# Softcap attention and FFN on one core: two token blocks go through the FFN in portions of 10 and 6 chunks

## The chip, the core and the metric

The kernel runs on 1 core of one Trainium2 chip. The metric is device time in microseconds (us) of one execution; the median of 3 runs of the kernel before is 713.72 us (710.97 to 714.97).

## The reference, cut to what matters

```python
# 4 batches, 12 heads, 448 positions, head size 64
scores = (q @ k.T) / sqrt(64)
scores = cap * tanh(scores / cap)              # cap = 30
attn   = exp(scores - max); attn /= attn.sum(-1) + 1e-9
x      = (attn @ v), heads side by side        # 1792 tokens x 768
h      = x @ w_in                              # w_in 768 x 2048, 64-bit floats
g      = h - tanh(h)
out    = g @ w_out                             # w_out 2048 x 768, 64-bit floats
```

The weights arrive as 64-bit floats and are decoded on the core. To keep 32-bit accuracy with fast matmuls, operands are split into a high and a low part, and a product is three matmuls (high x high, high x low, low x high).

## The kernel before, in words

The 1792 tokens are 4 blocks, one per batch, of 448 tokens; 384 of each (three tiles of 128) go through the FFN with their block, and the 64 that are left over of every block go through with block 3. The 12 heads are 6 pairs per block; a pair's attention (`prep_pair`, `scores`, `pv` or `pv_f32`, `normalize`, L513 to L890) ends in one 128-row slice of the block's transposed x. The first 11 pairs use plain 32-bit matmuls for attn @ v (`F32_PAIRS`, L32), which need no split of the exponentials; the other 13 split them.

The FFN of a block loops over 16 chunks of 128 hidden columns (`moe`, L1195). A chunk needs its weights: `prep_w` (L1070) calls `fetch_w` (L936), which in block 0 reads 1.5 MiB of raw 64-bit words (L965 and L977), decodes them with three VectorE passes (L1007, L1014, L1021) into a buffer `u`, and writes `u` to DRAM from the POOL queue (`fuk`, L951); the other blocks read `u` back, 768 KB (L944). Then `u` is split into `wi` and `wo`, each a copy (L420 on ScalarE or L422 on VectorE) and a subtraction (L431). `first` (L1109) makes 18 matmuls of 384 columns into h (L1124 to L1126), then tanh on ScalarE (L1137), h - tanh on VectorE (L1139) and a split of g. `second` (L1155) adds 18 matmuls (L1177) to the block's sums y, which stay in five PSUM banks over all its 16 chunks, with the `first` of the next chunk ahead of the `second` of this one. After the last chunk `store` (L1325) copies the sums to buffers `o` (two of them) and sends them out. `split_x` (L1084) makes the high and low parts of a block's x, `xh` and `xl`, at its first chunk; there are six buffers of each, as many as one block needs, so the next block's parts are written when the last `first` that reads the old ones is through. There are two buffers of raw words (`w64`), two of `u`, two of `wi`, three of `wo`, and six of `x`.

The order on every engine and DMA queue is written when the kernel is built: `Plan.schedule` (L119) places the operations one by one with a table of costs, prefers what can start at once, and among those the earliest due time. `emit` (L1366) gives the due times: FFN block b is due from `starts[b]`, and the attention of block b + 1 is spread over the time of FFN block b, moved ahead by `LEAD` (L34). So the attention of block 0 comes first and alone, and that of blocks 1, 2 and 3 stands between the matmuls of FFN blocks 0, 1 and 2. In blocks 2 and 3, `inspect` (L1027) reads the raw weights again to look at their range.

Of the kernel before, what the change touches and what calls it, by code (L numbers as in the profile page):

```python
# [31 lines left out]
F32_PAIRS = 11  # L32

LEAD = (18000.0, 30000.0, 20000.0, 20000.0)  # L34
# [267 lines left out]
class Build:  # L302
# [6 lines left out]
    def __init__(self, ctx, tc, q, k, v, w_in, w_out, out, consts, checks, general):  # L309
# [47 lines left out]
        self.raw, self.u, self.w, self.kept_op = {}, {}, {}, {}  # L357
        self.acc = {}
# [577 lines left out]
    def fetch_w(self, i):  # L936

        nc, DM, plan = self.nc, self.DM, self.plan
        m, f = divmod(i, self.NF)
        cols = slice(128 * f, 128 * f + 128)  # L940
        if m:
            u = plan.buf("u", [128, 2, DM])
            o = self.dma(
                "SP", 8 * 128 * DM, lambda: nc.sync.dma_start(out=u(), in_=self.u_kept[f]), [self.kept_op[f]], [u]  # L944
            )
            return u, [o]
# [123 lines left out]
    def prep_w(self, i):  # L1070

        DM = self.DM
        u, deps = self.fetch_w(i)
# [10 lines left out]
    def split_x(self, m):  # L1084
        n, plan = self.FULL, self.plan
        self.xa = []
        for d in range(self.ND):
            xh, xl = plan.buf("xh", [128, n], F32R), plan.buf("xl", [128, n], F32R)
            x, o = self.x.pop((m, d))
            ops = self.split(n, xh, xl, x, [o], ([xh], [xl]), ([x], [x, xh]))  # L1090
            self.xa.append((xh, xl, slice(0, n), ops))
        if m < self.B - 1:
            return
# [101 lines left out]
    def moe(self):  # L1195
# [4 lines left out]
        n = B * NF  # L1200
        for i in range(n + 1):
            m, f = divmod(i, NF)
            pm, pf = divmod(i - 1, NF)
            if i < n:
                self.prep_w(i)
# [5 lines left out]
                if f == 0:  # L1211
                    self.split_x(m)
                fifo[i] = []
                yield from self.first(self.w[i][0], self.xa, self.FULL, ("g", "gh", "gl"), fifo[i])
            if i > 0:
                yield from self.second(
                    self.w[i - 1][1], fifo[i - 1][0], [(0, 0), (1, 128), (2, 256)], pf == NF - 1
                )
                if pf == NF - 1:
                    self.store((0, 1) if pm == B - 1 else (0, 1, 2), pm)  # L1220
# [4 lines left out]
            if i > 0 and pm == B - 1:  # L1225
                yield from self.second(self.w[i - 1][1], fifo[i - 1][1], [(3, 0), (4, 128)], pf == NF - 1)
# [25 lines left out]
    def rest(self):  # L1252
# [3 lines left out]
        o4 = self.store((2, 3, 4), self.B - 1)  # L1256
# [68 lines left out]
    def store(self, tiles, m):  # L1325
        k = self.at + 3000
        for i in tiles:
            o = self.plan.buf({3: "eh", 4: "el"}.get(i, "o"), [128, self.DM])
            ops = []
            for bk, c0, e0, ne in self.PIECES[i]:  # L1330
                acc = self.acc[bk]
                new = not ops
                ops.append(
                    self.copy(
                        ne, lambda o=o, e0=e0, ne=ne: o()[:, e0 : e0 + ne],
# [141 lines left out]
```

## Time and profile before

| | |
|---|---|
| median of 3 runs | 713.72 us (710.97 to 714.97) |
| profiled execution, first to last instruction | 712.2 us |
| attention of block 0 alone, 0 to 78.7 us | PE busy 68.69 us of 78.70 |
| FFN block 0 with attention of block 1, to 240.4 us | PE busy 154.78 us of 161.70 |
| FFN block 1 with attention of block 2, to 387.1 us | PE busy 145.53 us of 146.70 |
| FFN block 2 with attention of block 3, to 533.9 us | PE busy 146.01 us of 146.80 |
| FFN block 3 and the left-over tokens, to the end | PE busy 172.34 us of 178.30 |

How to read the profile: PE is TensorE's matmuls, PEld its weight loads (they overlap), DVE is VectorE, ACT is ScalarE, POOL is GpSimd, SP the SyncE queue that issues most transfers; a q behind an engine's name is its queue of issues and waits. A group of instructions is named by its line, its engine and the tiles it writes and reads (`fwi<-fu` writes wi and reads u). Matmuls overlap in the records, so the distance between two starts is what one costs. The stages of the table begin with the first FFN matmul of each block. Idle time of an engine counts only where the matmuls wait for it.

### The profile page before, as it was taken

How to read it: one execution, taken by the hardware profiler on the slowest of the kernel's cores; microseconds unless marked ns; L12 is line 12 of the kernel's file. 1: busy time of each engine (PE TensorE's matmuls, PEld its weight loads, DVE VectorE, ACT ScalarE, POOL GpSimd, SP SyncE). 2: the span in 40 equal slices, each digit the busy share in tenths (PEclk: the TensorE clock that was granted, in tenths of full speed). 3: DMA queues.
4: the chain of work that ended last, by engine and by line, in shares of the span. 5: the costliest groups of instructions: out<-in, count | busy, mean ns of one | idle time of the engine just before them, and what ended most of it. 6: DMA issues, size and time to landing. Idle time of an engine off the chain costs nothing.

```text
span 712.2 us, 10004 instructions
## 1 busy us (share of the span) xinstructions
PE 687.4 (97%) x3624; PEld 603.2 (85%) x3624; DVE 515.2 (72%) x800; ACT 563.8 (79%) x961; POOL 14.3 (2%) x35
## 2 busy tenths in 40 slices
PE   6998999989999999999999999999999999999996
PEld 5655788778788888999999989899989999999996
DVE  5798999988999889877788888786694333333331
ACT  7998987848778999989989999999886655455553
POOL 2000000000000000000000000000000000000000
PEclk9999999999999999999999999999999999999999
DMA  6999899999974576653536785686676566676433
GB/s 102 152 212 194 191 285 241 225 250 243 266 263 137 111 206 172 170 125 97 120 95 176 233 205 153 157 219 180 166 212 227 154 141 167 178 166 152 133 84 116
DMA packets 156159, 125.96 MB, mean 177 GB/s; under 512 B 115268, under 2 KB 142020, under 8 KB 156100
## 3 DMA queue, kind: packets, MB, share of 16 engines
q1 hardware_dynamic: 153716, 112.58, 65.8%
q0 software_dynamic: 2304, 12.58, 4.9%
q8 instruction: 30, 0.49, 0.3%
q14 instruction: 29, 0.24, 0.1%
q10 hardware_dynamic: 80, 0.07, 0.0%
HBM read 107.12 MB, written 18.09 MB: 176 GB/s over the span
## 4 chain that ended last, share of the span: by engine, by line
PE 50%; ACT 25%; DVE 10%; DMA 10%; issue 3%; SPq 2%; DVEq 0%; ACTq 0%
PE facc L1177 16%; PE fh L1124 7%; DMA fw<-in_moe_w_in_dram 7%; PE fh L1126 7%; PE fh L1125 7%; PE fs L649 3%; ACT fqst L420 2%; ACT fe L722 2%; ACT fe L663 2%; ACT feh L663 2%; DMA fu<-fuk 2%; PE fp L790 2%; ACT fwi L420 2%; ACT feh L722 2%; ACT feh L420 2%
## 5 line engine op out<-in xcount | busy, mean ns | idle before, releaser
L1177 PE MATMUL facc<-fwo,fgh 128*128 128x512 f32 (+1 forms) x768 | 171.2, 345 | 0.0
L1177 PEld LDWEIGHTS facc<-fwo,fgh 128*128 128x128 f32 x768 | 127.4, 188 | 20.1 <-issue 5.8
L1124 PE MATMUL fh<-fxh,fwi 128*128 128x384 f32 x384 | 135.9, 354 | 0.0
L1126 PE MATMUL fh<-fxh,fwi 128*128 128x384 f32 x384 | 130.2, 339 | 0.3 <-DVE fwi L431 0.3
L1125 PE MATMUL fh<-fxl,fwi 128*128 128x384 f32 x384 | 128.8, 335 | 0.0
L1177 PE MATMUL facc<-fwo,fgl 128*128 128x512 f32 (+1 forms) x384 | 99.0, 339 | 0.0
L431 DVE TENSOR_TENSOR fwi<-fu,fwi 128x768 fp32r<-128x768 f32 x66 | 62.8, 952 | 48.8 <-ACT fwi L420 48.6
L420 ACT CAST fwi<-fu 128x768 fp32r<-128x768 f32 x62 | 51.7, 834 | 37.9 <-PE fh L1126 24.6
L1124 PEld LDWEIGHTS fh<-fxh,fwi 128*128 128x128 f32 x384 | 72.2, 188 | 5.6 <-issue 2.6
L1125 PEld LDWEIGHTS fh<-fxl,fwi 128*128 128x128 f32 x384 | 72.2, 188 | 4.5 <-issue 3.0
L431 DVE TENSOR_TENSOR fwo<-fu,fwo 128x768 fp32r<-128x768 f32 x66 | 62.6, 952 | 15.5 <-ACT fwo L420 15.1
L1126 PEld LDWEIGHTS fh<-fxh,fwi 128*128 128x128 f32 x384 | 72.0, 188 | 0.6 <-DVE fwi L431 0.6
L1139 DVE TENSOR_TENSOR fg<-fh,fg 128x384 f32<-128x384 f32 x64 | 35.6, 557 | 47.7 <-ACT fg L1137 46.7
L1177 PEld LDWEIGHTS facc<-fwo,fgl 128*128 128x128 f32 x384 | 58.7, 188 | 8.6
L649 PE MATMUL fs<-fqst,fkst 128*128 128x448 f32 x142 | 55.4, 411 | 4.7 <-DVE fkst L557 2.7
L1137 ACT ACTIVATE fg<-fh 128x384 f32<-128x384 f32 x64 | 31.2, 487 | 35.2 <-PE fh L1126 35.0
L663 ACT ACTIVATE fe<-fs 128x448 f32<-128x448 f32 x91 | 49.3, 541 | 7.7 <-PE fs L649 6.7
L431 DVE TENSOR_TENSOR fel<-fe,feh 128x896 fp32r<-128x896 f32 x39 | 42.4, 1087 | 12.3 <-ACT feh L420 12.2
L420 ACT CAST feh<-fe 128x896 fp32r<-128x896 f32 (+1 forms) x64 | 50.7, 794 | 0.6
L722 ACT ACTIVATE fe<-fe,absc 128x896 f32<-128x896 f32 (+1 forms) x52 | 49.6, 954 | 0.6
L420 ACT CAST fwo<-fu 128x768 fp32r<-128x768 f32 x56 | 46.4, 829 | 4.0 <-PE facc L1177 3.7
L649 PE MATMUL fs<-fql,fkz 128*128 128x448 f32 x124 | 45.5, 367 | 0.0
(191 smaller groups left out, 1329.6 us busy)
## 6 DMA issues: line engine op xcount, KB each, us to landing
fu<-fuk SPq DMA_DIRECT2D x48, 768.0 KB
fw<-in_moe_w_in_dram SPq DMA_DIRECT2D x64, 384.0 KB
fw<-in_moe_w_out_dram SPq DMA_DIRECT2D x32, 768.0 KB
fuk<-fu POOLq DMA_DIRECT2D x16, 768.0 KB, 5.9
fqraw<-in_q_dram SPq DMA_DIRECT2D x44, 112.0 KB
fkraw<-in_k_dram SPq DMA_DIRECT2D x44, 112.0 KB
out_dram<-fo SPq DMA_DIRECT2D x12, 384.0 KB
fvraw<-in_v_dram SPq DMA_DIRECT2D x26, 96.0 KB
```

Source lines behind the costliest of these rows:

```text
L420: self.nc.scalar.copy(out(), in_())
L431: lambda: self.nc.vector.tensor_sub(lo(), x(), hi().bitcast(F32)),
L649: nc.tensor.matmul(ps()[:, :S], k, q, start=n == 0, stop=n == passes - 1)
L663: S, lambda: nc.scalar.activation(dst(), ps()[:, :S], AF.Tanh), [o],
L722: lambda e=e, w=w: nc.scalar.activation(e()[:, :w, :], e()[:, :w, :], AF.Exp, scale=self.absc),
L790: nc.tensor.matmul(P()[:, :S], self.v_block(v1(), hp, c), e()[:, j, :], start=n == 0, stop=n == 3)
L1124: nc.tensor.matmul(h()[:, :n], wh, ah, start=(d == 0), stop=False)
L1125: nc.tensor.matmul(h()[:, :n], wh, al, start=False, stop=False)
L1126: nc.tensor.matmul(h()[:, :n], wl, ah, start=False, stop=(d == ND - 1))
L1137: n, lambda: nc.scalar.activation(g()[:, :n], h()[:, :n], AF.Tanh), [prev], [g], [h], psum=True, key=k
L1139: o = self.dve(n, lambda: nc.vector.tensor_sub(g()[:, :n], h()[:, :n], g()[:, :n]), [o], [], [g, h], key=k + 600)
L1177: nc.tensor.matmul(banks[bk]()[:, c0 : c0 + ne], lhs()[:, ts], w()[:, k, e0 : e0 + ne], start=bk in firsts and bk not in begun, stop=stop ...
```

## The change

`SEGMENTS` replaces the loop over blocks: chunks 0 to 9 of block 0, chunks 0 to 9 of block 1, chunks 10 to 15 of block 0, chunks 10 to 15 of block 1, then blocks 2 and 3 whole. Weights of chunk f are decoded where f comes up first. When block 0 or 1 leaves off after chunk 9, its sums go to DRAM (`keep_y`: the copies of `store`, then three SP transfers of 384 KB), and they come back into `o` at its end, where VectorE adds them to the sums in PSUM (`evict` with `old`). Its xh and xl are written to DRAM by 12 POOL transfers of 192 KB when they are made (`keep_x`), and read back by 12 SP transfers when it goes on (`fetch_x`). `SHARES` says beside which portions the attention is due: that of block 1 beside the first, of block 2 half beside the second and half beside the third, of block 3 beside block 2. `LEAD` has a value for each portion. The buffers are as before.

```diff
--- before.py
+++ after.py
@@ -31,7 +31,11 @@
 
 F32_PAIRS = 11
 
-LEAD = (18000.0, 30000.0, 20000.0, 20000.0)
+SEGMENTS = ((0, 0, 10), (1, 0, 10), (0, 10, 16), (1, 10, 16), (2, 0, 16), (3, 0, 16))
+
+SHARES = (None, {0: 1.0}, {1: 0.5, 2: 0.5}, {4: 1.0})
+
+LEAD = (18000.0, 40000.0, 30000.0, 30000.0, 30000.0, 30000.0)
 
 FREE_PAIRS = 8
 
@@ -355,6 +359,15 @@
         self.x, self.xt_ops = {}, {d: [] for d in range(self.ND)}
         self.raw_qk, self.ready, self.raw_v = {}, {}, {}
         self.raw, self.u, self.w, self.kept_op = {}, {}, {}, {}
+        self.segments = [(m, a, z) for m, a, z in SEGMENTS]
+        later = {m for m, a, _ in self.segments if a}
+        self.x_kept = {
+            m: [self.dram.tile([128, 2, self.FULL], F32, name=f"{nm}xk{m}_{d}") for d in range(self.ND)] for m in later
+        }
+        self.y_kept = {
+            m: [self.dram.tile([128, self.DM], F32, name=f"{nm}yk{m}_{i}") for i in range(3)] for m in later
+        }
+        self.x_ops, self.y_ops = {}, {}
         self.acc = {}
         self.at = 0.0
         if not general:
@@ -933,12 +946,10 @@
 
 
 
-    def fetch_w(self, i):
+    def fetch_w(self, f):
 
         nc, DM, plan = self.nc, self.DM, self.plan
-        m, f = divmod(i, self.NF)
-        cols = slice(128 * f, 128 * f + 128)
-        if m:
+        if f in self.kept_op:
             u = plan.buf("u", [128, 2, DM])
             o = self.dma(
                 "SP", 8 * 128 * DM, lambda: nc.sync.dma_start(out=u(), in_=self.u_kept[f]), [self.kept_op[f]], [u]
@@ -1067,10 +1078,10 @@
         o = self.plan.op("PL", 2000.0, spread, [o], key=k)
         self.plan.op("D", 70.0, put, [o], key=k)
 
-    def prep_w(self, i):
+    def prep_w(self, i, f):
 
         DM = self.DM
-        u, deps = self.fetch_w(i)
+        u, deps = self.fetch_w(f)
         made = []
         for j, tag in enumerate(("wi", "wo")):
             w = self.plan.buf(tag, [128, 2, DM], F32R)
@@ -1081,14 +1092,43 @@
             made.append((w, list(ops)))
         self.w[i] = made
 
-    def split_x(self, m):
+    def fetch_x(self, m, d):
+
+        n, plan, nc, kept = self.FULL, self.plan, self.nc, self.x_kept[m][d]
+        both = [plan.buf(t, [128, n], F32R) for t in ("xh", "xl")]
+        ops = [
+            self.dma(
+                "SP", 512 * n, lambda j=j, t=t: nc.sync.dma_start(out=t().bitcast(F32), in_=kept[:, j, :]), self.x_ops[m, d], [t],
+            )
+            for j, t in enumerate(both)
+        ]
+        return (*both, slice(0, n), ops)
+
+    def keep_x(self, m, d):
+
+        n, nc, kept = self.FULL, self.nc, self.x_kept[m][d]
+        *both, _, ops = self.xa[d]
+        self.x_ops[m, d] = [
+            self.dma(
+                "PL", 512 * n, lambda j=j, t=t: nc.gpsimd.dma_start(out=kept[:, j, :], in_=t().bitcast(F32)), [ops[j]], [], [t],
+                key=self.at + 40000,
+            )
+            for j, t in enumerate(both)
+        ]
+
+    def split_x(self, m, again, more):
         n, plan = self.FULL, self.plan
         self.xa = []
         for d in range(self.ND):
+            if again:
+                self.xa.append(self.fetch_x(m, d))
+                continue
             xh, xl = plan.buf("xh", [128, n], F32R), plan.buf("xl", [128, n], F32R)
             x, o = self.x.pop((m, d))
             ops = self.split(n, xh, xl, x, [o], ([xh], [xl]), ([x], [x, xh]))
             self.xa.append((xh, xl, slice(0, n), ops))
+            if more:
+                self.keep_x(m, d)
         if m < self.B - 1:
             return
         n = self.B * self.TAIL
@@ -1197,33 +1237,37 @@
         NF, B = self.NF, self.B
         fifo = {}
         self.acc_op = {}
-        n = B * NF
+        steps = [(m, f, a, z) for m, a, z in self.segments for f in range(a, z)]
+        n = len(steps)
         for i in range(n + 1):
-            m, f = divmod(i, NF)
-            pm, pf = divmod(i - 1, NF)
             if i < n:
-                self.prep_w(i)
+                m, f, a, z = steps[i]
+                self.prep_w(i, f)
                 if m >= B - 2 and f % 2 == 0 and not self.general:
                     c = (m - B + 2) * NF // 2 + f // 2
                     self.inspect(c)
                     if c == NF - 1:
                         self.verdict()
-                if f == 0:
-                    self.split_x(m)
+                if f == a:
+                    self.split_x(m, a > 0, z < NF)
                 fifo[i] = []
                 yield from self.first(self.w[i][0], self.xa, self.FULL, ("g", "gh", "gl"), fifo[i])
             if i > 0:
+                pm, pf, pa, pz = steps[i - 1]
+                end = pf == pz - 1
                 yield from self.second(
-                    self.w[i - 1][1], fifo[i - 1][0], [(0, 0), (1, 128), (2, 256)], pf == NF - 1
+                    self.w[i - 1][1], fifo[i - 1][0], [(0, 0), (1, 128), (2, 256)], end
                 )
-                if pf == NF - 1:
-                    self.store((0, 1) if pm == B - 1 else (0, 1, 2), pm)
+                if end and pz < NF:
+                    self.keep_y(pm)
+                elif end:
+                    self.store((0, 1) if pm == B - 1 else (0, 1, 2), pm, pa > 0)
             if i < n and m == B - 1:
                 tags = ("rb", ("kT", "qT")[f % 2], ("num", "sumT")[f % 2])
                 yield from self.first(self.w[i][0], self.xb, B * self.TAIL, tags, fifo[i])
                 self.stash(f, fifo[i][1])
             if i > 0 and pm == B - 1:
-                yield from self.second(self.w[i - 1][1], fifo[i - 1][1], [(3, 0), (4, 128)], pf == NF - 1)
+                yield from self.second(self.w[i - 1][1], fifo[i - 1][1], [(3, 0), (4, 128)], end)
             if i > 0:
                 del fifo[i - 1], self.w[i - 1]
         yield from self.rest()
@@ -1253,7 +1297,7 @@
 
         nc, NF, plan = self.nc, self.NF, self.plan
         groups, others = self.w_rest(), self.acc_op[6]
-        o4 = self.store((2, 3, 4), self.B - 1)
+        o4 = self.store((2, 3, 4), self.B - 1, False)
         acc = plan.buf("h")
         prev = None
         for n, (fs, w, ops) in enumerate(groups):
@@ -1322,21 +1366,53 @@
                 groups.append((fs, w, ops))
         return groups
 
-    def store(self, tiles, m):
-        k = self.at + 3000
-        for i in tiles:
-            o = self.plan.buf({3: "eh", 4: "el"}.get(i, "o"), [128, self.DM])
-            ops = []
-            for bk, c0, e0, ne in self.PIECES[i]:
-                acc = self.acc[bk]
-                new = not ops
+    def keep_y(self, m):
+
+        nc, k, self.y_ops[m] = self.nc, self.at + 3000, []
+        for i in (0, 1, 2):
+            o, ops = self.evict(i, self.plan.buf("o", [128, self.DM]), (), k)
+            self.y_ops[m].append(
+                self.dma(
+                    "SP", 512 * self.DM, lambda i=i, o=o: nc.sync.dma_start(out=self.y_kept[m][i], in_=o()), ops, [], [o],
+                    key=self.at + 20000,
+                )
+            )
+        self.acc, self.acc_op = {}, {}
+
+    def evict(self, i, o, old, k):
+
+        nc, ops = self.nc, []
+        for bk, c0, e0, ne in self.PIECES[i]:
+            acc = self.acc[bk]
+            new = not ops
+            to, of = (lambda e0=e0, ne=ne: o()[:, e0 : e0 + ne]), (lambda acc=acc, c0=c0, ne=ne: acc()[:, c0 : c0 + ne])
+            if old:
                 ops.append(
-                    self.copy(
-                        ne, lambda o=o, e0=e0, ne=ne: o()[:, e0 : e0 + ne],
-                        lambda acc=acc, c0=c0, ne=ne: acc()[:, c0 : c0 + ne], [self.acc_op[bk]],
-                        [o] if new else [], [acc] if new else [acc, o], psum=True, key=k,
+                    self.dve(
+                        ne, lambda to=to, of=of: nc.vector.tensor_add(to(), of(), to()), [self.acc_op[bk], *old],
+                        [], [acc, o], key=k,
                     )
                 )
+                continue
+            ops.append(
+                self.copy(
+                    ne, to, of, [self.acc_op[bk]], [o] if new else [], [acc] if new else [acc, o], psum=True, key=k,
+                )
+            )
+        return o, ops
+
+    def store(self, tiles, m, kept):
+        k, nc = self.at + 3000, self.nc
+        for i in tiles:
+            o, old = self.plan.buf({3: "eh", 4: "el"}.get(i, "o"), [128, self.DM]), []
+            if kept:
+                old = [
+                    self.dma(
+                        "SP", 512 * self.DM, lambda i=i, o=o: nc.sync.dma_start(out=o(), in_=self.y_kept[m][i]),
+                        [self.y_ops[m][i]], [o], key=self.at - 5000,
+                    )
+                ]
+            o, ops = self.evict(i, o, old, k)
             self.put(i, m, o, ops, slice(0, 512 if i == 4 else self.DM))
         for bk in {pc[0] for i in tiles for pc in self.PIECES[i]}:
             del self.acc[bk], self.acc_op[bk]
@@ -1367,14 +1443,23 @@
 
 
         NP, NF = self.NP, self.NF
-        lead = NP * (15 * SCORE + 8 * FULL32) if F32_PAIRS and not self.general else NP * 37 * SCORE
-        block = NF * (18 * COLS[384] + 9 * (COLS[512] + COLS[256]))
-        share = {}
-        starts = [lead]
+        lead = NP * (15 * SCORE + (8 * FULL32 if F32_PAIRS and not self.general else 22 * SCORE))
+        chunk = 18 * COLS[384] + 9 * (COLS[512] + COLS[256])
+        share, own = {}, [(z - a) * chunk for _, a, z in self.segments]
         for b in range(1, self.B):
             f32 = max(0, min(NP, F32_PAIRS - b * NP)) if not self.general else 0
             share[b] = NP * 15 * SCORE + f32 * 8 * FULL32 + (NP - f32) * 22 * SCORE
-            starts.append(starts[-1] + share[b] + block)
+        starts = [lead]
+        for k, t in enumerate(own):
+            starts.append(starts[-1] + t + sum(s * share[b] for b in share for j, s in SHARES[b].items() if j == k))
+
+        def due(b, part):
+
+            for k, s in SHARES[b].items():
+                if part <= s + 1e-6 or k == max(SHARES[b]):
+                    t0, t1 = starts[k] - LEAD[k], starts[k + 1] - LEAD[k + 1]
+                    return t0 + (t1 - t0) * (part / s if s else 1.0)
+                part -= s
 
         done, b = 0.0, 0
         gen = self.attention()
@@ -1390,21 +1475,20 @@
             if b == 0:
                 self.at = done * (lead - LEAD[0]) / lead
             elif b < self.B:
-                a0, a1 = starts[b - 1] - LEAD[b - 1], starts[b] - LEAD[b]
-                self.at = a0 + done * (a1 - a0) / share[b]
+                self.at = due(b, done / share[b])
             else:
                 self.at += c
-        done, b = 0.0, 0
+        done, k = 0.0, 0
         self.at = starts[0]
         for c in self.moe():
             done += c
-            while b < self.B - 1 and done >= block:
-                done -= block
-                b += 1
-            if b < self.B - 1:
-                self.at = starts[b] + done * (starts[b + 1] - starts[b]) / block
+            while k < len(own) - 1 and done >= own[k]:
+                done -= own[k]
+                k += 1
+            if k < len(own) - 1:
+                self.at = starts[k] + done * (starts[k + 1] - starts[k]) / own[k]
             else:
-                self.at = starts[b] + done
+                self.at = starts[k] + done
         self.plan.run(SETTINGS[:1] if self.general else SETTINGS)
 
 
```

## Rows read from the trace of the kernel before

**Rows 1.** Busy time by stage; us, then busy (instructions) of each engine, clock, DMA share, GB/s

```profile
0.00:78.70 78.70, 68.69 (x226) 46.16 (x226) 63.22 (x121) 72.16 (x125) 5.42 (x18) 0.98 0.92 164
78.70:240.40 161.70, 154.78 (x758) 129.99 (x757) 151.38 (x195) 124.97 (x212) 8.51 (x16) 1.00 0.94 234
240.40:387.10 146.70, 145.53 (x788) 133.53 (x787) 119.83 (x187) 134.75 (x229) 0.00 (x0) 1.00 0.53 138
387.10:533.90 146.80, 146.01 (x786) 132.71 (x785) 118.09 (x196) 137.95 (x223) 0.00 (x0) 1.00 0.71 191
533.90:712.20 178.30, 172.34 (x1076) 160.84 (x1074) 62.71 (x105) 93.93 (x176) 0.35 (x1) 1.00 0.57 151
sum 712.20, PE 687.35 PEld 603.24 DVE 515.23 ACT 563.77 POOL 14.29; mean PE 137.47 PEld 120.65 DVE 103.05 ACT 112.75 POOL 2.86
```

**Rows 2.** Timeline of PE where blocks begin: start, us, line and operation, [idle before]

```profile
78.69 0.69 PE L1124 MATMUL fh<-fxh,fwi 128*128 128x384 f32 x1
...
239.78 0.54 PE L649 MATMUL fs<-fqst,fkst 128*128 128x448 f32 x1 [1.53 <-ACT fe L663]
...
240.36 0.34 PE L1124 MATMUL fh<-fxh,fwi 128*128 128x384 f32 x1
...
242.47 0.37 PE L649 MATMUL fs<-fqst,fkst 128*128 128x448 f32 x1
...
387.07 0.33 PE L1124 MATMUL fh<-fxh,fwi 128*128 128x384 f32 x1
...
530.74 0.86 PE L1177 MATMUL facc<-fwo,fgh 128*128 128x512 f32 x4
...
533.87 0.34 PE L1124 MATMUL fh<-fxh,fwi 128*128 128x384 f32 x1
```

**Rows 3.** Groups of DVE, 78.7 to 240.4 us: count, busy us, mean ns, idle before

```profile
L1021 DVE SCALAR_TENSOR_TENSOR fu<-fw,fu 128x1536 uint32<-128x1536 uint32 x14 | 24.5, 1747 | 0.2
L1014 DVE SCALAR_TENSOR_TENSOR fu<-fw,fu 128x1536 uint32<-128x1536 uint32 x14 | 24.4, 1746 | 0.1
L431 DVE TENSOR_TENSOR fwo<-fu,fwo 128x768 fp32r<-128x768 f32 x16 | 15.2, 947 | 0.2 <-ACT fwo L420 0.2
L431 DVE TENSOR_TENSOR fwi<-fu,fwi 128x768 fp32r<-128x768 f32 x15 | 14.2, 949 | 1.6 <-ACT fwi L420 1.6
L1007 DVE TENSOR_SCALAR fu<-fw 128x1536 uint32<-128x1536 uint32 x14 | 13.3, 951 | 5.0 <-DMA fw<-in_moe_w_in_dram 5.0
L1139 DVE TENSOR_TENSOR fg<-fh,fg 128x384 f32<-128x384 f32 x16 | 8.9, 556 | 1.8 <-ACT fg L1137 1.3
L431 DVE TENSOR_TENSOR fgl<-fg,fgh 128x384 fp32r<-128x384 f32 x15 | 8.1, 542 | 0.0
```

**Rows 4.** Groups of ACT, 240.4 to 387.1 us, columns as in rows 3

```profile
L420 ACT CAST fwi<-fu 128x768 fp32r<-128x768 f32 x17 | 14.2, 833 | 0.9 <-DMA fu<-fuk 0.8
L420 ACT CAST fwo<-fu 128x768 fp32r<-128x768 f32 x14 | 11.6, 832 | 3.7 <-PE facc L1177 3.5
L420 ACT CAST fgh<-fg 128x384 fp32r<-128x384 f32 x17 | 8.7, 510 | 0.8 <-DVE fg L1139 0.8
L1137 ACT ACTIVATE fg<-fh 128x384 f32<-128x384 f32 x16 | 7.7, 483 | 0.1
L420 ACT COPY fo<-facc 128x512 f32<-128x512 f32 (+1 forms) x6 | 2.6, 486 | 0.0
```

**Rows 5.** The page's bandwidth in 40 slices of 17.8 us

```profile
GB/s 102 152 212 194 191 285 241 225 250 243 266 263 137 111 206 172 170 125 97 120 95 176 233 205 153 157 219 180 166 212 227 154 141 167 178 166 152 133 84 116
```

**Rows 6.** Chain of waits in order of time, two reads of u: start, us

```profile
227.75 6.62 DMA fu<-fuk
...
249.18 5.75 DMA fu<-fuk
```

**Rows 7.** Groups of POOL, and line L944 on SP (issue ns, least/median/most)

```profile
L951 POOL DMA_DIRECT2D fuk<-fu x16 | 8.8, 553 | 206.4 <-DVE fu L1021 177.0 <-DVE fr L866 17.7 <-DMA fw<-in_moe_w_out_dram 11.6
...
L944 SPq DMA_DIRECT2D fu<-fuk x48: 319/327/2133, 227.8 to 657.1; - x48
```

## The prediction, made before the change was run

> **What bounds the kernel now.** I read the busy time by stage first [rows 1]. TensorE's matmuls (PE) are busy 687.4 of 712.2 us, so only 24.9 us can be won at all, and it matters where they lie. 10.0 us are in the lead, where the attention of block 0 stands alone, and 6.0 us after the last matmuls; the change touches neither. FFN block 0 has 161.70 - 154.78 = 6.9 us, FFN block 1 has 1.2 us, block 2 has 0.8 us. The stage that the change aims at, the one with the decoding, holds no more than 6.9 us.
>
> There the second view shows what is short. VectorE (DVE) is busy 151.4 us, 98% of PE's busy time, with ACT at 81%. In the next stage DVE is at 82% and ACT at 93%, and PE idles only 0.8% [rows 1]. Decoding costs DVE 24.5 + 24.4 + 13.3 = 62.2 us for 14 chunks [rows 3], 4.44 us each (two more were decoded in the lead). The rest of a chunk costs it 0.95 + 0.95 + 0.56 + 0.54 = 3.0 us [rows 3], and ACT 0.83 + 0.83 + 0.51 + 0.48 = 2.66 us [rows 4].
>
> PE's share comes from the timeline [rows 2]: 12 first-pass matmuls from 240.36 to 242.47, so 3.16 us for 18, and a second pass from 530.74 to 533.87; together 6.3 us a chunk. What is left of a stage is its six pairs of heads. In the first stage DVE has (151.4 - 62.2 - 16 x 3.0) / 6 = 6.9 us per pair, PE (154.8 - 16 x 6.3) / 6 = 9.0. In the second, where the exponentials are split, DVE has (119.8 - 48) / 6 = 12.0, ACT (134.8 - 16 x 2.66) / 6 = 15.4, PE (145.5 - 100.8) / 6 = 7.45. So a chunk with decoding asks DVE for 7.44 us against 6.3 us of matmuls, a later pair for 12.0 against 7.45, and a plain chunk for 3.0 against 6.3. The plain chunks are what pays for the other two, and the change moves them about.
>
> **First portion (block 0, chunks 0 to 9, all of block 1's attention).** Six chunks leave. PE keeps 154.8 - 6 x 6.3 = 117.0 us, DVE 151.4 - 6 x 7.44 = 106.8 (91% of PE), ACT 125.0 - 6 x 2.66 = 109.0 (93%). DVE's ratio lies 9/16 of the way from the second stage (82%, idle 0.8%) to the first (98%, idle 4.5%), so I take 2.9% of 117 us, 3.4 us idle in place of 6.9: a gain of 3.5 us. Bounds: 6.0 us if it runs as the second stage does, nothing if ACT, now as full as DVE, takes DVE's place.
>
> **Second portion (block 1, chunks 0 to 9).** Plain chunks beside block 2's attention, as in the second stage, only with more attention to a chunk. I take its idle share and no change; cover is ten plain chunks.
>
> **Third portion (block 0, chunks 10 to 15, decoding).** With one pair of block 2 left for it, DVE has 6 x 7.44 + 12.0 + 3.3 (the additions, below) = 59.9 us against 6 x 6.3 + 7.45 = 45.3 of PE. The two buffers of u and wi let two chunks be decoded and split ahead, 2 x (4.44 + 1.9) = 12.7 us, if the second portion leaves DVE the time. Then 47.2 against 45.3 stays, 1.9 us over, and the idle share of 4.5% that the first stage had at such a ratio gives 2.0 more [rows 1]: 4 us lost. Bounds: nothing, if attention falls behind its due time into the fourth portion (six plain chunks, 18 us of DVE for 38 of PE); 19.2 us with two pairs left and nothing done ahead (71.9 against 52.7).
>
> **Two more seams.** At each, `xh` and `xl` come by 12 SP transfers, whose buffers come free only as the last first pass reads them; SP waits for that, and behind the waiting transfers stand the raw words, u and q, k, v of what follows. The two seams now between portions cost 1.53 us (239.78) and nothing (387.07) [rows 2]; I take the mean, 0.75 us each, 1.5 us. The 12 transfers are 2304 KB, three reads of u. At the page's best slice, 285 GB/s [rows 5], their 2.36 MB take 8.3 us, and at the pace of single reads of u, 5.75 to 6.62 us [rows 6], up to 19.9 us. Cover is two second passes, 6.3 us, the first pass as it starts (2.1 us), and any attention that is ready. So a seam costs between nothing and 19.9 - 8.4 = 11.5 us. On SP itself a further 36 issues (24 of x, 12 of y) are 0.33 us each at the median [rows 7], 12 us over the span, off the path.
>
> The Trainium skill speaks against such transfers ("DMA: Bandwidth & Descriptors", section "Bandwidth"): it wants them batched to 1 MiB or more, and these are 192 KB. An estimate by the Trainium skill's fit there, 2.0 us and 436 GB/s, is 7.4 us for the twelve overlapped, which the cover hides, and 29 us one after the other; for one read of u the same fit gives 3.8 us, where the trace has 5.75 to 6.62, so the rows decide.
>
> **Sums and writes of x.** Keeping y adds 12 copies, 0.49 us at the mean [rows 4], 5.8 us beside the next first pass, as at every block's end now. The 12 additions have a nearest row in L1139, which reads PSUM too: 0.56 us for 384 columns [rows 3], so 1.1 us per tile of 768, 3.3 us per block. What can stand on the path is the third tile: with two buffers `o` its old sums can be read only when the first tile has been sent, two transfers in series, perhaps 8 us against about 5 us until the next second pass wants the bank. I take 0.5 us for both ends, between nothing and 6. POOL issues 24 more transfers of 0.55 us [rows 7]; it waited 206 us for work, so they hide, and they would cost only if raw words come later for them: DVE's three waits for those were 5.0 us [rows 3], and I let none to 5 us stand for it. The new due times shift the lead's order too: none, 2 us either way.
>
> **The sum.** -3.5 + 4 + 1.5 + 0.5 = +2.5 us, so a span of 714.7. The median of the runs is 1.5 us above this execution's span, so I predict 716 us. A measurement of this kernel can tell 0.5%, 3.6 us, from no change: 710.2 to 717.3 counts as the same.
>
> **Rivals.** *Even load, faster.* From the lead's end to block 2 the DVE and ACT work together hardly grows, so if attention slides off the third portion into the plain chunks, the 300 us of PE's work there may idle as the second stage does, 0.8%, 2.4 us in place of 6.9 + 1.2 = 8.1. With seams that hide, 712.2 - 5.7 = 706.5 of span, 708. For it: in the second stage that load was carried. Against it: u and wi let nothing be decoded more than two chunks ahead.
>
> *The decoding comes back, slower.* The place is the third portion, the engine DVE. It decides from more than one pair of block 2 left there: with 1.5 pairs and one chunk done ahead, 65.9 - 6.3 = 59.6 us of DVE against 49.0, 10.6 us lost, and 4.5% more, 2.2: +12.8 in place of +4, 725 us. For it: half of block 2's attention is due beside that portion. Against it: it is due 30 us before the portion ends.
>
> *Transfers, slower.* Decoding six chunks moves 6 x 2304 KB = 14.2 MB; less 3.1 MB read ahead, with 2.4 MB of x and 2.4 MB of y it is some 16 MB in 47 us, 340 GB/s, where no slice shows more than 285 [rows 5]. At 285 it takes 56 us: +9 us, 725. Against it: no stage was held by bandwidth alone, and the writes can lag.
>
> *Seams that stall, slower.* If the x transfers go at the pace of single reads of u, three times 5.75 us less the cover of 8.4 is 8.9 us a seam: 716 - 1.5 + 17.8 = 732. Against it: transfers overlap elsewhere, and attention fills such waits. The Trainium skill's rule of 1 MiB (the section named above) points the same way; the trace bears out that its transfers are slow, not that they would stand alone.
>
> *It does nothing*, if ACT, at 93% in both, takes back what DVE gives in the first portion and the third loses nothing: 714.
>
> **Chances.** The forecast, with that last one, 0.36; even load 0.29; decoding 0.20; transfers 0.09; seams 0.06. So faster 0.29, the same 0.36, slower 0.35. The forecast's own range is 711 to 717. Over all, 705 to 727 takes in the even load and the two cases at 725 and leaves out the seams and the ends of the bounds.
>
> **What would show it.** Right: idle of PE in the first portion at 3 to 4 us; in the third portion DVE busier than PE, and gaps of PE behind `fwi` or `fu`; gaps of 1 us where portions meet. Wrong: the third portion without gaps (then attention went elsewhere, and the time is under 712), or PE waiting for `fxh` or `fxl` from DRAM by several us.

## The result, and the profile after

The changed kernel takes 717.39 us (median of 8 runs, 715.12 to 720.47) against 712.84 us (707.97 to 715.39) for the kernel before in the same runs: a ratio of 1.0079, 95% interval 1.0050 to 1.0107. Measured twice more below it came to 1.0050 (1.0006 to 1.0093) and 1.0084 (1.0049 to 1.0118). It is slower, by a little over the 0.5% of the prediction. Medians and ratios, here and below, leave out the few executions that lay more than 1.5% above the fastest of their kernel.

The busy time by stage of the changed kernel: the lead, the four portions, block 2, block 3 and the rest (columns as in [rows 1]).

```profile
0.00:75.00 75.00, 70.43 (x230) 48.59 (x231) 63.76 (x132) 69.07 (x120) 7.95 (x23) 0.98 0.95 171
75.00:197.80 122.80, 118.57 (x536) 95.76 (x535) 114.83 (x157) 110.15 (x189) 13.56 (x26) 0.97 1.01 252
197.80:287.90 90.10, 89.62 (x485) 81.86 (x485) 76.68 (x112) 79.39 (x134) 3.22 (x6) 1.00 0.63 177
287.90:344.90 57.00, 54.31 (x290) 48.25 (x289) 51.82 (x67) 42.07 (x74) 2.13 (x4) 1.00 0.88 246
344.90:392.60 47.70, 45.80 (x249) 40.98 (x248) 36.06 (x57) 36.48 (x62) 0.00 (x0) 1.00 0.74 236
392.60:537.50 144.90, 142.32 (x769) 129.46 (x768) 115.21 (x190) 129.77 (x209) 0.00 (x0) 1.00 0.66 189
537.50:715.90 178.40, 172.41 (x1076) 160.86 (x1074) 61.75 (x104) 93.59 (x177) 0.36 (x1) 0.99 0.55 156
sum 715.90, PE 693.45 PEld 605.77 DVE 520.12 ACT 560.52 POOL 27.22; mean PE 99.06 PEld 86.54 DVE 74.30 ACT 80.07 POOL 3.89
```

Set beside [rows 1]: the lead is 3.7 us shorter; blocks 0 and 1 take 317.6 us (the four portions) against 308.4, 9.2 more; block 2 takes 1.9 less, the tail the same. Together that is 3.7 us, by which the span grew. Of the 9.2, as it happens, 3.7 us too are work that only changed place: PE's busy time in block 2 fell from 146.01 to 142.32, because the new `LEAD` has the attention of block 3 due earlier. So blocks 0 to 2 are best read as one stretch: 455.2 us before, 462.5 after.

Three things are odd in these rows. The first portion has PE's clock at 0.97. VectorE, which was to be short in the third portion, is busy there 51.82 us and PE 54.31. And the fourth portion, plain chunks with little attention, idles 1.9 us. The page's bandwidth and its DMA totals show a fuller memory (the page of before has 125.96 MB and a mean of 177 GB/s):

```profile
GB/s 102 155 223 197 318 215 247 241 228 225 279 249 191 103 97 234 276 257 195 294 268 179 219 187 174 171 160 183 194 203 275 158 136 171 177 177 135 152 68 115
DMA packets 162879, 140.12 MB, mean 196 GB/s; under 512 B 116228, under 2 KB 146052, under 8 KB 162820
```

**The end of the first portion.** The chain of waits from 169 to 191 us (start, us, what):

```profile
170.06 0.87 SPq L976
...
170.97 0.61 SPq L988
...
177.95 9.70 DMA fu<-fuk
...
187.66 0.84 ACT fwi L433
...
188.53 0.96 DVE fwi L444
189.49 1.01 DVE fel L444
...
190.54 0.74 PE fp L832
```

L976 and L988 are raw words: those of chunk 10, which the third portion decodes from 262.7 us on. As the two `w64` buffers come free of chunks 8 and 9, SP fetches chunk 10 (issued 169.3 to 172.2 us) and chunk 11 (179.2 to 181.2 us). The first read of `u` for block 1 goes out between them, at 177.95, and takes 9.70 us, where two reads of before took 6.62 and 5.75 [rows 6]. It is late twice over: in e6 below, where these raw words come later, SP issues the same read at 173.68, although its first portion begins only 0.8 us earlier, and it is there when ScalarE comes to it.

```profile
173.68 20.29 SPq L963 DMA_DIRECT2D fu<-fuk  x3
```

In the changed kernel ScalarE stands 4.29 us before its copy of `fwi`, as its order has that copy ahead of the attention's. PE's clock in stretches of 5 us, first of after, then of before at its own seam:

```profile
180.00:185.00 5.00, 5.00 (x27) 4.28 (x27) 4.67 (x10) 3.30 (x6) 0.00 (x0) 1.00 1.04 293
185.00:190.00 5.00, 3.25 (x17) 2.52 (x15) 1.47 (x2) 2.31 (x4) 0.00 (x0) 1.00 1.06 210
190.00:195.00 5.00, 4.51 (x14) 3.85 (x14) 4.29 (x9) 4.97 (x12) 3.53 (x7) 0.50 1.02 259
195.00:200.00 5.00, 5.00 (x25) 4.55 (x24) 4.14 (x7) 1.59 (x5) 2.81 (x6) 0.82 0.83 275
```

```profile
235.00:240.00 5.00, 3.47 (x20) 2.75 (x19) 4.07 (x8) 4.92 (x11) 0.00 (x0) 1.00 1.15 196
240.00:245.00 5.00, 5.00 (x28) 4.86 (x29) 3.20 (x7) 4.90 (x10) 0.00 (x0) 1.00 0.54 113
```

Behind the gap (1.75 us, and 0.49 us soon after) PE's granted clock is 0.50, that is 1.2 GHz, through 190 to 195 us and into the next stretch; at before's seam, with a gap of 1.53 us [rows 2], it stayed at 1.00. The gap is idle time; the half clock hides in "busy".

**The third and fourth portions.** PE's waits (times, then the longest), first from 287.9 to 344.9 us, then to 392.6:

```profile
PE fh L1166 <- DVE fwi L444: 0.8, 1, 0.8
PE fp L832 <- DVE fel L444: 0.7, 1, 0.7
PE fh L1165 <- DMA fxl<-fxk: 0.5, 1, 0.5
PE fh L1164 <- ACT fwi L433: 0.5, 1, 0.5
...
PE fh L1164 <- DVE fg L1179: 1.7, 1, 1.7
```

and the chain around the step from the one to the other:

```profile
335.99 7.20 DMA fu<-fuk
...
343.21 0.85 ACT fwi L433
...
345.65 7.00 DMA fu<-fuk
...
352.67 0.84 ACT fwi L433
...
353.54 0.96 DVE fwi L444
354.50 0.48 DVE fg L1179
```

The third portion waits in four small places; of x by 0.5 us. At the end of it two reads of `u` come one after the other, 7.20 and 7.00 us, and feed chunks of 6.3 us. Between the two, in the order written for SP, stand x's 12 reads. The issue of the first and last of them, and then of the second read of `u` in e3 below, which leaves x's transfers out (its first went out at 332.54):

```profile
337.36 0.34 SPq L1101 DMA_DIRECT2D fxh<-fxk  x1
...
345.07 0.36 SPq L1101 DMA_DIRECT2D fxl<-fxk  x1
```

```profile
336.22 0.34 SPq L957 DMA_DIRECT2D fu<-fuk  x1
```

So the second read goes out 9.7 us after the first, but 3.7 us after it without x, and then PE does not wait as long for it (0.9 us in place of 1.7). The first takes no less without x (7.50 us in e3).

### The profile page after: what moved, and what is told of

Same layout as the page of the kernel before. It is cut to its first block, busy times and chain, and to the rows that moved or that the text cites. A ratio compares the mean times of both kernels' runs of the same rounds, so it can differ in the third digit from the quotient of the medians.

```text
span 715.9 us, 10135 instructions
## 1 busy us (share of the span) xinstructions
PE 693.5 (97%) x3624; PEld 605.8 (85%) x3624; DVE 520.1 (73%) x813; ACT 560.5 (78%) x960; POOL 27.2 (4%) x59
## 4 chain that ended last, share of the span: by engine, by line
PE 49%; ACT 18%; DMA 15%; DVE 11%; SPq 3%; issue 2%; DVEq 0%; ACTq 0%
PE facc L1217 17%; DMA fw<-in_moe_w_in_dram 8%; PE fh L1164 7%; PE fh L1166 7%; PE fh L1165 7%; DMA fu<-fuk 4%; PE fs L662 3%; DMA fvraw<-in_v_dram 2%; PE fp L1217 2%; PE fs L1217 2%; PE fp L803 2%; ACT feh L676 1%; ACT feh L735 1%; DVE fwo L444 1%; DVE fwi L444 1%
## 5 line engine op out<-in xcount | busy, mean ns | idle before, releaser
L662 PE MATMUL fs<-fqst,fkst 128*128 128x448 f32 x142 | 59.0, 436 | 4.1 <-ACT fkst L433 2.2
L433 ACT CAST fwo<-fu 128x768 fp32r<-128x768 f32 x59 | 48.9, 829 | 8.2 <-PE facc L1217 7.7
L444 DVE TENSOR_TENSOR fgl<-fg,fgh 128x384 fp32r<-128x384 f32 x64 | 35.4, 553 | 17.5 <-ACT fgh L433 17.1
```

What stands on the lines that cost most here:

```text
L433: self.nc.scalar.copy(out(), in_())
L444: lambda: self.nc.vector.tensor_sub(lo(), x(), hi().bitcast(F32)),
L662: nc.tensor.matmul(ps()[:, :S], k, q, start=n == 0, stop=n == passes - 1)
```

## Experiments

e1, e3 and e5 to e10 keep the changed kernel's own order on every engine and queue; only what is named leaves it or is moved. e2 and e4 are planned anew. Every kernel ran 12 times beside the kernel before on the same chip.

**e1: the raw words of chunks 10 and 11 later.** They move on SP to just ahead of the sixth and seventh read of `u` (the edit without its helpers).

```diff
...
+        if f in (10, 11) and not self.general:
+            self.plan.moves.append((ops, self.u_ops[f - 5]))
```

> The changed kernel with the order of every engine kept and one thing moved on the SP queue: the raw words of chunks 10 and 11, which the changed kernel reads at 169 to 181 us although they are decoded only from 262 us on, are read after the seam, ahead of the reads of u for chunks 5 and 6 of block 1. Theory A (the early raw reads share the transfers with the first read of u, which then takes 9.7 us, holds ACT 4.3 us and PE 2.2 us and drops the clock to 1.2 GHz for 6.8 us): that read lands in 6 to 7 us, the half clock goes, and the time falls by 3 to 5 us against the changed kernel, to a ratio of 1.001 to 1.004 to the kernel before. Theory B (the seam itself, two buffers of u that come free late, is the cause): nothing changes, ratio 1.007 to 1.009.

715.80 us, ratio 1.0037 (1.0006 to 1.0068). In its profile PE has no wait of over 0.5 us left at the end of the first portion, but the execution (span 720.2 us) lost as much elsewhere: as the portion began, a read of v took 12 us.

```profile
PE fp L809 <- DMA fv1float<-in_v_dram: 4.8, 1, 4.8
```

```profile
76.43 11.99 DMA fv1float<-in_v_dram
```

This profile alone proves little, as e8, which lost 5.0 us in the same way, has no gap at the end of the portion either, with the raw words early. But e4, e6 and e9, with the raw words later and no loss of that size, have none over 0.5 us there, and e3, with the raw words early, has it. So the gap is the raw words' doing, and the time of e1 doesn't show it by itself.

**e2: the new due times alone**, in the kernel before.

```diff
-LEAD = (18000.0, 30000.0, 20000.0, 20000.0)
+LEAD = (18000.0, 40000.0, 30000.0, 30000.0)
```

> The kernel before, blocks whole, with the due times alone taken over (lead of the first four values 18000, 40000, 30000, 30000). Theory A (the 5.2 us that the changed kernel wins before its first FFN matmul come from the attention's due times): the first FFN matmul falls to about 75 us and the time to 706 to 709 us, ratio 0.992 to 0.996. Theory B (they come from the chunks that stand further apart, 11.5 us in place of 9.5, since block 1's attention lies beside ten chunks): the lead stays at 78 to 79 us and the ratio within 0.996 to 1.004.

713.63 us, ratio 1.0016 (0.9986 to 1.0047): no change. The profile's lead (span 709.1 us) is 73.3 us long, so the shorter lead comes from the due times and not from the cut, and block 2's PE share falls in the same way as in the changed kernel. Block 0, whole and with all its decoding, idles 3.7 us there, where before has 6.9:

```profile
0.00:73.30 73.30, 65.89 (x223) 45.72 (x223) 62.77 (x124) 67.95 (x117) 4.88 (x17) 1.00 0.91 160
73.30:233.40 160.10, 156.44 (x760) 130.91 (x761) 155.75 (x202) 129.41 (x218) 9.67 (x17) 1.00 1.01 241
...
382.60:530.50 147.90, 143.22 (x771) 129.96 (x770) 115.44 (x190) 131.48 (x215) 0.00 (x0) 1.00 0.66 184
```

**e3: x not written and not read back.** The 24 writes and 24 reads are left out; chunks 10 to 15 of a block use the x that is in the buffers, so that their waits for free buffers go too.

```diff
...
-                "SP", 512 * n, lambda j=j, t=t: nc.sync.dma_start(out=t().bitcast(F32), in_=kept[:, j, :]), self.x_ops[m, d], [t],
+                "SP", 512 * n, lambda: None, self.x_ops[m, d], [t],
...
-                "PL", 512 * n, lambda j=j, t=t: nc.gpsimd.dma_start(out=kept[:, j, :], in_=t().bitcast(F32)), [ops[j]], [], [t],
+                "PL", 512 * n, lambda: None, [ops[j]], [], [t],
```

> The changed kernel with the order of every engine kept and the 48 transfers of x's parts to and from DRAM left out: chunks 10 to 15 of block 0 are computed on the parts of block 1's x, which are still in their buffers. Theory A (the transfers of x cost time at the seams and slow the reads of u beside them): the stall on xl and half of the 1.8 us stall behind the late u at the fourth portion go, 1.5 to 3 us less than the changed kernel, ratio 1.003 to 1.006. Theory B (they are hidden by second passes and attention): less than 1 us, ratio 1.007 to 1.009.

715.06 us, ratio 1.0041 (1.0005 to 1.0076). The last two portions take 54.4 and 46.0 us in place of 57.0 and 47.7; the gaps at the end of the first portion remain, behind the same kind of work:

```profile
PE fp L832 <- DVE fsumT L862: 1.9, 1, 1.9
PE fp L832 <- ACT feh L435: 1.2, 1, 1.2
```

**e4: one cut.** Block 0 alone is cut at chunk 10, block 1 goes through whole, and the raw words are held until block 1 is at its fifth chunk.

```diff
-SEGMENTS = ((0, 0, 10), (1, 0, 10), (0, 10, 16), (1, 10, 16), (2, 0, 16), (3, 0, 16))
+SEGMENTS = ((0, 0, 10), (1, 0, 16), (0, 10, 16), (2, 0, 16), (3, 0, 16))
-SHARES = (None, {0: 1.0}, {1: 0.5, 2: 0.5}, {4: 1.0})
+SHARES = (None, {0: 1.0}, {1: 0.75, 2: 0.25}, {3: 1.0})
...
```

> Only block 0 is cut: chunks 0 to 9 of block 0, block 1 whole (it decodes chunks 10 to 15), then chunks 10 to 15 of block 0; block 2's attention is due three quarters beside block 1 and one quarter beside the rest of block 0, and the raw words of chunks 10 and 11 wait until block 1 is at its fifth chunk. One seam and half of the kept x and y less. Theory A (the seams are what the change pays): 3 to 7 us less than the changed kernel, ratio 0.998 to 1.004. Theory B (VectorE short of time where the six chunks are decoded is what it pays): the gaps stay at those chunks, ratio 1.004 to 1.009.

714.69 us, ratio 1.0025 (0.9993 to 1.0058): between the two kernels and told apart from neither. Block 0 coming back still waits (2.0 us behind `fg`, 0.7 us for x).

**e5: the changed kernel again**, to see which of its gaps recur.

> The changed kernel itself once more, beside the other three of this group, for a second profile and as the time to compare them with. Theory A (the stall at the first seam is a matter of its order of transfers): the first read of u takes 8 us or more again and PE waits 1.5 us or more there; ratio 1.005 to 1.010. Theory B (one late transfer that could have come anywhere, as the read of v that took 12 us at 76 us in the run with the raw words read later): the seam is clean this time and a gap of that size stands elsewhere; the ratio is the same.

715.84 us, ratio 1.0050 (1.0006 to 1.0093). Both do; PE's longest waits in the first portion and from 287.9 us on:

```profile
PE fp L830 <- ACT feh L433: 2.9, 1, 2.9
...
PE fh L1164 <- DVE fg L1179: 2.6, 1, 2.6
```

The read of `u` ahead of the first took 9.74 us here, 9.70 in the profile above and 9.65 in e10.

**e6: raw words later and no x**, the edits of e1 and e3 together.

> The changed kernel with the order of every engine kept, the raw words of chunks 10 and 11 read after the seam, and the transfers of x's parts left out (chunks 10 to 15 of block 0 are computed on block 1's x). Theory A (late transfers are all that the change pays, and the cut itself wins some us): the time falls below both runs with one of the two, 4 to 7 us less than the changed kernel, ratio 0.998 to 1.002, the last four portions as in the run without x. Theory B (something else, VectorE in the third portion or the seams as such, costs what is left): ratio 1.003 to 1.006.

712.12 us, ratio 0.9989 (0.9955 to 1.0023): level with the kernel before, and 3.7 us under e5, where theory A had 4 to 7. Its lead, portions and block 2:

```profile
0.00:74.20 74.20, 68.81 (x231) 46.68 (x232) 63.73 (x132) 69.05 (x120) 4.88 (x17) 1.00 0.92 159
74.20:192.70 118.50, 115.51 (x536) 93.57 (x535) 114.13 (x157) 109.97 (x189) 5.87 (x11) 1.00 0.90 212
192.70:283.80 91.10, 90.18 (x484) 81.78 (x483) 77.07 (x111) 79.06 (x134) 1.06 (x2) 1.00 0.68 185
283.80:338.20 54.40, 53.34 (x289) 48.36 (x289) 51.10 (x68) 41.74 (x73) 2.13 (x4) 1.00 0.76 227
338.20:384.40 46.20, 45.13 (x250) 41.29 (x249) 36.28 (x57) 36.69 (x63) 0.00 (x0) 1.00 0.69 203
384.40:529.50 145.10, 142.37 (x770) 129.51 (x769) 115.19 (x190) 129.76 (x209) 0.00 (x0) 1.00 0.67 189
```

The ratio's interval still meets that of e5. The first portion is 4.3 us shorter than in the changed kernel, with 3.06 us less of PE's busy time for the same 536 matmuls (no half clock) and 1.2 us less idle. Its reads of `u` from 165 to 195 us, by the list of DMA issues (KB each, median us to landing), and all that the memory moved in that time:

```profile
DMA packets 7327, 4.27 MB, mean 142 GB/s; under 512 B 6794, under 2 KB 6794, under 8 KB 7323
...
fu<-fuk SPq DMA_DIRECT2D x3, 768.0 KB, 4.4
```

In the changed kernel 8.97 MB were moved from 165 to 200 us, a mean of 256 GB/s, and a read took 9.70 us.

**e7: x's writes spread.** As e1, with the writes on SP one tile at a time beside later transfers, and nothing left out.

```diff
...
+                lambda j=j, t=t: (nc.gpsimd if self.general else nc.sync).dma_start(out=kept[:, j, :], in_=t().bitcast(F32)),
...
+            for m, d in self.x_ops:
+                self.plan.moves.append((self.x_ops[m, d], (self.u_ops if m else self.raw_ops)[3 + d]))
```

> The whole computation, the changed kernel's order on every compute engine, with the raw words of chunks 10 and 11 read after the seam and the 24 writes of x's parts taken from POOL and put into the SP queue two by two, ahead of the raw words of chunks 3 to 8 and of the reads of u for chunks 3 to 8 of block 1. Theory A (the burst of 12 writes makes the transfers beside it late): 2 to 4 us less than the changed kernel, ratio 1.001 to 1.004, no gap behind a read of v or u at 75 to 90 us and at 185 to 200 us. Theory B (it is the reads of x that cost, and the writes are hidden): as the run with the raw words read later, ratio 1.003 to 1.006.

718.69 us, ratio 1.0073 (1.0032 to 1.0115): no gain, and above what either theory had. That the burst of the writes costs is not shown; nor is it ruled out, as the edit also puts 24 issues on SP ahead of raw words and reads of `u`. x's reads stand where they stood, and the gap of the fourth portion stays (3.3 us behind `fg`).

**e8: short decoding.** Two of the three VectorE passes are left out for chunks 10 to 15, 2 x 1.75 us each.

```diff
...
-            lambda: nc.vector.scalar_tensor_tensor(
+            lambda: None if less else nc.vector.scalar_tensor_tensor(
...
```

> The changed kernel with the order of every engine kept and two of the three VectorE passes of the decoding left out for chunks 10 to 15 (their weights are not the right ones), 3.5 us of VectorE less per chunk, 21 us in all. Theory A (the transfers of x hold the third and the fourth portion): PE's gaps there stay within 1 us of the changed kernel's, ratio 1.006 to 1.009. Theory B (the prediction's: VectorE is short of time in the third portion): the gaps behind VectorE there go, 2 to 4 us less, ratio 1.002 to 1.005.

716.43 us, ratio 1.0046 (1.0006 to 1.0086): in theory B's range, but so is e5, which leaves nothing out. The third portion now has not one wait of PE (busy 52.80 of 52.80 us), the fourth has its gap as before:

```profile
289.00:341.80 52.80, 52.80 (x290) 48.58 (x290) 39.23 (x60) 42.44 (x74) 2.13 (x4) 1.00 0.88 255
341.80:391.60 49.80, 46.72 (x249) 42.68 (x248) 35.89 (x56) 36.40 (x62) 0.00 (x0) 0.97 0.72 224
```

```profile
PE fh L1164 <- DVE fg L1179: 3.0, 1, 3.0
```

The two portions together last 102.6 us, against 104.7 in the changed kernel: 21 us of VectorE's work in them and ahead of them (6 x 3.5) taken away win 2.1 us. VectorE is not what the change waits for in the main: the third portion's waits are VectorE's, but without them PE waits for `u` in the fourth.

**e9 and e10: the kernel of e6 and the changed kernel, side by side**, since only e6 stood clear of the first measurement of the changed kernel, and might have been scatter.

> The kernel of e6 once more (raw words of chunks 10 and 11 read behind the first seam, x's 48 transfers left out), beside the changed kernel in the same runs. Theory (the transfers that the cut adds or lets come early are what it pays for): again within 2.5 us of the kernel before, and 3 to 6 us under the changed kernel of e10. Rival (e6 was scatter; the cut pays for VectorE and the seams themselves): 715 us or more, within 2 us of e10.

> The changed kernel unaltered, so that e9 is measured beside it. Both theories: 3 to 5 us over the kernel before, with gaps of PE of 2 to 3 us behind a late read of u near 187 us and near 351 us in the profile.

e9 took 713.72 us, ratio 1.0020 (0.9997 to 1.0043); e10 717.3 us, ratio 1.0084 (1.0049 to 1.0118): 3.6 us apart and with intervals that do not meet, as the theory of the transfers has it. The gap at the end of the first portion was smaller than expected in e10 (1.2 us behind `feh`, another 1.9 us behind `fsumT`), that of the fourth was 2.4 us. The stages from rows like the ones above, of the changed kernel's three profiles, of those without x's transfers and of the two with whole blocks (e1, e7 and e8 have other losses besides, e4 other portions):

| us | before | e2 | changed | e5 | e10 | e3 | e6 | e9 |
|---|---|---|---|---|---|---|---|---|
| lead | 78.7 | 73.3 | 75.0 | 74.5 | 75.0 | 75.4 | 74.2 | 74.9 |
| first portion | | | 122.8 | 123.3 | 122.8 | 121.6 | 118.5 | 117.8 |
| third and fourth | | | 104.7 | 104.9 | 104.5 | 100.4 | 100.6 | 100.8 |
| blocks 0 to 2 | 455.2 | 457.2 | 462.5 | 461.2 | 461.3 | 456.3 | 455.3 | 457.2 |

With x's transfers out and the raw words later, blocks 0 to 2 take what they took before the change, or with the new due times alone. Within the 2 us that such profiles differ by, the cut itself gains nothing there and loses nothing.

## Why the prediction came out as it did

The time was right (716 us, range 705 to 727, against 717.39), and so was the sign of its likeliest sum (+2.5 us, measured +3.7 of span). But 717.39 lies just past the 717.3 that it still called the same, and by the ratio the outcome is the one it gave 0.35, "slower". Its sum came close because two errors met: it had +2.5 us in blocks 0 and 1 and nothing elsewhere; the trace has +9.2 there, and -3.7 in the lead and -1.9 in block 2.

**First portion, -3.5.** The size came where the raw words are later: in e6 it idles 118.50 - 115.51 = 3.0 us, where the prediction had 3.4 and before had 6.9. The reason given, less decoding beside it, is not shown. In e2 block 0 keeps all 14 decodings, VectorE is busy 155.75 us to PE's 156.44, a fuller ratio than in before, and PE idles 160.10 - 156.44 = 3.7 us: by these single profiles the due times alone bring most of it, and VectorE's share does not by itself set the idle time. In the changed kernel the gain was eaten: 4.2 us idle and 3.06 us of half clock. The step that failed is the account of the raw words: the prediction saw in "Two more seams" that they stand on SP behind the x transfers, and in the rival "Transfers" it counted the 3.1 MB of chunks 10 and 11 read ahead as relief for the third portion. It didn't ask when they would be read. Free buffers let them go 90 us early, ahead of the read that feeds the first plain chunk and beside it.

**Second portion, 0.** It idles 0.5 us of 90.1. Right.

**Third portion, +4.** Too large, and the reason held only in part. Only four of its six chunks are decoded in it:

```profile
L1018 DVE TENSOR_SCALAR fu<-fw 128x1536 uint32<-128x1536 uint32 x4 | 3.8, 958 | 2.1 <-DMA fw<-in_moe_w_in_dram 2.0
```

The second portion, with VectorE at 76.68 of 90.10 us, took the other two, as the prediction allowed. The mark that it set, VectorE busier than PE, did not come. PE idles 2.7, 1.4 and 1.2 us there in the three profiles, 1.1 without x (e3, e6 and e9) and nothing with short decoding: about 1 us is VectorE's, and the rest varies from one execution to the next.

**Two more seams, +1.5.** This is the term that was too small. The bounds were right to reach to 11.5 us, but the cost was looked for in PE waiting for `fxh` and `fxl`, and that is 0.5 and 0.2 us. x's reads make another one late instead. The prediction had that too, "behind the waiting transfers stand the raw words, u", but priced a seam by x's transfers alone, less their cover, and not by what stands behind them: the second read of `u`, which went out 6 us later than it does without x. That its place behind x's reads is what costs is read from the rows; no run moves it. Without x (e3) the third and fourth portions are 4.3 us shorter, and without early raw words as well the first is another 3.1 us shorter (e6 against e3). By rows the two together are 5.4 us of blocks 0 to 2 (461.7 us, the mean of the changed kernel's three profiles, less 456.3, that of e6 and e9), by the medians of the two pairs 3.7 (e5, e6) and 3.6 (e10, e9). How the sum divides is less sure: by themselves neither e1 nor e3 differs from the changed kernel by more than the scatter.

**Sums kept, +0.5.** PE waits nowhere on the additions or the copies of y in the changed kernel. The 12 additions took 551 ns at the mean, close to the 556 ns that stood for them.

**Lead and block 2, 0.** In the profile the lead is 3.7 us shorter, from the due times (e2), where the bounds were 2 us either way. It is kept in no median: e2 is level with before, so part of the lead of 78.7 us may be that one execution's.

**The rivals.** "Even load" (0.29) did not come in the changed kernel; its load is even, as the second and third portions show, and what it lacked is its condition, "seams that hide". In e6 and e9, where they hide, the time is that of before and not the 708 us that the rival gave: PE idles 6.0 us in e6's four portions in place of 2.4. "Decoding comes back" (0.20) falls with e8, although its condition was met: about two pairs of block 2 lay in the third portion (they ended at 302 and 323 us, a third at 361). "Transfers" (0.09) took 285 GB/s for the most that there is; a slice of the changed kernel shows 318. The third portion moved 246 GB/s and wasn't held by the total. "Seams that stall" (0.06) had the right place and too high a price.

The Trainium skill ("DMA: Bandwidth & Descriptors", section "Anatomy of one DMA — SWDGE (gpsimd) path", and not "Bandwidth" as the prediction has it) fits one transfer by 2.0 us and 436 GB/s. It says so of transfers issued from GpSimd, and the reads of `u` are SP's. The estimate of 3.8 us for such a read was set aside in the prediction for the 5.75 to 6.62 us of its rows. In e6 three reads have a median of 4.4 us where little else moves, so the fit is near there; beside the reads of before more was moving (190 to 215 GB/s in all).

## What to carry to other kernels

Ask of every transfer that a change makes possible earlier when it will now go, and what is read beside it: a prefetch that nobody needs for 90 us stood ahead of the one read that the engines waited for, and ran beside it. Spilling operands to DRAM to even out an engine's load was paid here in late reads at the seams, which show as waits for other tiles than the spilled ones: look at what stands behind the new transfers on the queue. And cut a kernel's time by stretches that hold the same work: due times had moved attention across a stage's border, and that alone looked like 3.7 us.

## What the runs showed that was not expected

Gaps of much the same length were followed by the half clock or not. In the changed kernel 1.75 us without work at 187 us were (0.50 from 190 to 195 us), and the matmuls behind them took some 3 us longer, more than the gap; at the same place e5 had 2.90 us and then 0.66, e10 1.20 us and then 1.00. At the gap of the fourth portion 1.67 us left the clock at 1.00, while 2.63 us (e5) and 2.39 us (e10) were followed by 0.68 and 0.83 from 355 to 360 us.

And a read of v as the first portion begins, small but late, cost 4.8 and 5.0 us of PE in the profiles of e1 and e8, while x's writes were going out. It did so in none without these writes (e3, e6, e9), but nor did it in the three of the changed kernel, which has them, and PE waits 1.8 us for v in the lead of e2, which writes no x. That the writes are its cause is not shown.
